# First layer of two in steps of one feature tile and a whole batch: wide y products and a block for the remaining tokens

## The chip, the cores and the metric

One core of a Trainium2 chip runs the whole program. The metric is the device time of one execution in microseconds. The kernel before took 1465.08 us (median of 3 runs, 1463.18 to 1466.22).

## What is computed

An attention with few keys in between, then two feed-forward layers:

```python
p_packed = softmax(p k^T / 8) v          # 8 batches, 8 heads, 32 packed rows, 576 tokens, 64 wide
out      = softmax(q p_packed^T / 8) p_packed
x  = out as [8*576, 512]
h1 = x @ w_in1                           # [4608, 512] x [512, 2048]
g1 = h1 - tanh(h1)
y  = g1 @ w_out1                         # [4608, 2048] x [2048, 512]
h2 = y @ w_in2
out = (h2 * cos(h2)) @ w_out2
```

The weights arrive as 64-bit values and are joined on the chip. Every large product is made from three: each operand is split into a rounded part (hi) and the remainder (lo), and hi*hi, lo*hi and hi*lo are added up in PSUM.

## The kernel before

**The first layer** never forms x. With the packed attention's second softmax `a` (32 keys for each of 8 heads, 576 tokens of a batch, `a2` in two halves) the layer's input product is `a` times `g`, where `g` is the packed values times `w_in1` (`gmat`, L521: 32 small products for a quarter c of the features, split by `gsplit_hi` and `gsplit_lo`, L540 and L547). A step n is one entry of the list `steps` (L1158): a block of 288 tokens (half a batch) and two tiles of 128 features. Its parts:

- `h1` (L564): 12 products of 288 columns on TensorE into one of two PSUM tiles `h` of two banks each. All attention pieces use the same two tiles.
- ScalarE: tanh `t` and square `u` of h (L588, L589), then `y` (L632) and the mask `k` (L635). Both feature tiles go through one instruction of 576 columns.
- VectorE: `t` = h - tanh (L637), `d` = u*h (L638), `gl` of the step before (L659), the polynomial `y` (L640), and a masked copy of `t` into `y` (L644). The result is g.
- ScalarE rounds g to `gh` in the next step (L652).
- `ymm1` (L661): 24 products of 288 columns, two steps later: 4 output tiles d, 2 feature tiles, 3 products. They add up in four PSUM banks over 8 steps, the 2048 features of a block.

The first four blocks go through the first half of the features and then through the second (`NP`, `HS`), with the half-sums stored to memory and added on VectorE (`ypart1` L683, `yload` L692, `yevac1` L699); so only half of the weights is needed early. Later blocks are evacuated by ScalarE, four times 288 columns (L709).

**What sets the order.** Each engine runs its queue in order. Up to step 14 the queues follow the list `START` (L39), partly left to the scheduler; then a loop (L1194) issues each step in the order of the code, with tables that say in which step which other piece stands: attention of the batch to come (`attention`, `ATT`, `PACK`, `G`, L72 to L75: scores in steps 0 and 1 of 16, transposes in 2 and 4, values in 3 and 5, the pack in 7, second scores in 8 and 10, gp groups in 9, 11, 13 and 15), joins of second-layer weights (`CONV2`, L64) and their sums (`SUM1`, L67, `combine_ops` L853). `GLENG` (L37) says which of the first 15 `gl` GpSimd takes.

**The second layer** begins with one block of 512 tokens: `h2` (L726) of the pair `ORDER2[0]` stands between the last two `ymm1` (L1261 to L1265), its cosine on ScalarE and VectorE beside the last y products. It then goes on for 8 steps and for pairs of blocks with fewer, combined products. All its products have 512 columns. Loads and stores are issued on SP's queue, in order.

The lines that say what a step is:

```python
steps = [(blk, HS * h + s) for h in range(2) for blk in range(NP) for s in range(HS)]
steps += [(blk, s) for blk in range(NP, NB) for s in range(NSTEP)]
```

## Time and profile before

| | us |
|---|---|
| median of 3 runs | 1465.08 |
| profiled execution | 1464.91 |
| its span, first to last instruction | 1463.1 |
| TensorE busy | 1419.1 |
| TensorE weight loads busy | 1238.8 |
| VectorE busy | 1226.7 |
| ScalarE busy | 987.8 |
| GpSimd busy | 125.1 |

The profile is of one execution. Busy time of TensorE contains the overlap of pipelined products, so the pace is read from the start of one group to the start of the next. The weight loads run beside the products. DVE is VectorE, ACT ScalarE, POOL GpSimd, PE TensorE, PEld its weight loads, SP the engine that issues the DMAs. The first layer reaches to about 760 us.

### The profile page before, as it was taken

How to read it: one execution, taken by the hardware profiler on the slowest of the kernel's cores; microseconds unless marked ns; L12 is line 12 of the kernel's file. 1: busy time of each engine (PE TensorE's matmuls, PEld its weight loads, DVE VectorE, ACT ScalarE, POOL GpSimd, SP SyncE). 2: the span in 40 equal slices, each digit the busy share in tenths (PEclk: the TensorE clock that was granted, in tenths of full speed). 3: DMA queues.
4: the chain of work that ended last, by engine and by line, in shares of the span. 5: the costliest groups of instructions: out<-in, count | busy, mean ns of one | idle time of the engine just before them, and what ended most of it. 6: DMA issues, size and time to landing. Idle time of an engine off the chain costs nothing.

```text
span 1463.1 us, 26436 instructions
## 1 busy us (share of the span) xinstructions
PE 1419.1 (97%) x9964; PEld 1238.8 (85%) x9964; DVE 1226.7 (84%) x1707; ACT 987.8 (68%) x1548; POOL 125.1 (9%) x102
## 2 busy tenths in 40 slices
PE   5899999999999999999999999999999999999998
PEld 2688989999899998999998888878887888788887
DVE  6898797898989889899867679997889689868975
ACT  4887666778787776878875566654665566646752
POOL 0311010111211111121130000000000000000000
PEclk6899999999999999999999999999999999999999
DMA  9742455737557583565679557787768776887566
GB/s 358 268 178 64 140 173 161 248 109 252 172 177 250 167 268 127 211 213 188 196 270 402 193 189 236 244 245 211 209 189 257 220 211 192 243 237 211 173 171 181
DMA packets 205119, 307.47 MB, mean 210 GB/s; under 512 B 48256, under 2 KB 135296, under 8 KB 204992
## 3 DMA queue, kind: packets, MB, share of 16 engines
q1 hardware_dynamic: 203904, 305.52, 64.8%
q8 instruction: 79, 1.29, 0.4%
q14 instruction: 48, 0.39, 0.1%
q10 hardware_dynamic: 1088, 0.26, 0.1%
HBM read 238.35 MB, written 67.37 MB: 209 GB/s over the span
## 4 chain that ended last, share of the span: by engine, by line
PE 89%; DVE 4%; DMA 4%; issue 2%; ACT 1%; SPq 0%; POOL 0%; DVEq 0%; POOLq 0%; ACTq 0%
PE y L673 26%; PE p L996 21%; PE y L1006 13%; PE h L573 13%; PE p L1006 5%; PE h L734 3%; PE y L810 3%; PE gp L530 2%; DMA st<-w1i 1%; DMA yw<-wso 1%; PE pp L406 1%; DMA v<-vv 1%; PE s L338 1%; DMA q<-qT 1%; PE sc L338 1%
## 5 line engine op out<-in xcount | busy, mean ns | idle before, releaser
L996 PE MATMUL p<-b,hw 128*128 128x512 f32 x1302 | 308.1, 389 | 0.0
L673 PE MATMUL y<-gh,w1o 128*128 128x288 f32 x2048 | 303.9, 300 | 3.7 <-DVE ye L703 2.3
L673 PEld LDWEIGHTS y<-gh,w1o 128*128 128x128 f32 x2048 | 278.3, 189 | 29.9 <-ACT t L588 14.9
L996 PEld LDWEIGHTS p<-b,hw 128*128 128x128 f32 x1302 | 244.3, 188 | 51.0 <-DVE hb L1013 0.3
L573 PE MATMUL h<-a,g 128*128 128x288 f32 x1536 | 227.3, 297 | 6.7 <-DVE g L549 4.2
L573 PEld LDWEIGHTS h<-a,g 128*128 128x128 f32 x1536 | 212.9, 190 | 8.8 <-issue 7.2
L588 ACT ACTIVATE t<-h 128x576 f32<-128x576 f32 x113 | 73.7, 652 | 145.9 <-PE h L573 145.9
L673 PE MATMUL y<-gl,w1o 128*128 128x288 f32 x1024 | 156.4, 294 | 0.0
L673 PEld LDWEIGHTS y<-gl,w1o 128*128 128x128 f32 x1024 | 143.1, 188 | 0.8 <-DVE u L450 0.4
L1006 PE MATMUL y<-yh,yw 128*128 128x512 f32 x376 | 120.0, 391 | 3.8 <-DMA yw<-wso 2.6
L659 DVE TENSOR_TENSOR gl<-y,gh 128x576 fp32r<-128x576 f32 x125 | 105.9, 847 | 3.5 <-ACT gh L652 3.4
L644 DVE COPY_PREDICATED y<-k,t 128x576 f32<-128x576 int16 x113 | 95.2, 842 | 10.7 <-DVE y L640 0.5
L637 DVE TENSOR_TENSOR t<-h,t 128x576 f32<-128x576 f32 x113 | 84.0, 744 | 21.7 <-ACT u L589 21.0
L1013 DVE TENSOR_TENSOR yl<-k,yh 128x1024 fp32r<-128x1024 f32 x72 | 86.7, 1214 | 17.7 <-ACT yh L1016 17.1
L652 ACT ACTIVATE gh<-y 128x576 fp32r<-128x576 f32 x128 | 88.1, 688 | 10.0 <-DVE y L644 5.4
L1006 PE MATMUL y<-gh,yw 128*128 128x512 f32 x256 | 91.1, 389 | 0.0
L1006 PEld LDWEIGHTS y<-yh,yw 128*128 128x128 f32 x376 | 70.6, 188 | 21.3 <-ACT o L1016 2.4
L1016 ACT ACTIVATE c<-p 128x512 f32<-128x512 f32 x96 | 56.9, 593 | 43.8 <-PE p L996 43.8
L640 DVE SCALAR_TENSOR_TENSOR y<-y,d 128x576 f32<-128x576 f32 x113 | 85.8, 759 | 0.0
L638 DVE TENSOR_TENSOR d<-u,h 128x576 f32<-128x576 f32 x113 | 83.9, 742 | 0.0
L1006 PE MATMUL p<-yh,yw 128*128 128x512 f32 x256 | 80.8, 389 | 0.5 <-DMA yw<-wso 0.5
L632 ACT ACTIVATE y<-u 128x576 f32<-128x576 f32 x113 | 77.2, 684 | 0.0
(186 smaller groups left out, 2389.3 us busy)
## 6 DMA issues: line engine op xcount, KB each, us to landing
yw<-wso SPq DMA_DIRECT2D x128, 256.0 KB, 3.1
hw<-wsi SPq DMA_DIRECT2D x124, 256.0 KB, 3.1
w1i<-w1d SPq DMA_DIRECT2D x48, 512.0 KB, 5.4
yw<-wod SPq DMA_DIRECT2D x96, 256.0 KB, 3.3
hw<-wid SPq DMA_DIRECT2D x93, 256.0 KB, 3.3
y<-ye SPq DMA_DIRECT2D x80, 144.0 KB, 1.9
st<-w1i SPq DMA_DIRECT2D x16, 512.0 KB, 8.1
v<-vv SPq DMA_DIRECT2D x16, 512.0 KB, 6.7
```

The source lines that it names most:

```text
L573: nc.tensor.matmul(out=h[:, x, 0:HB], lhsT=gw[b, f // 4, half][:, ga, c0:c0 + 128], rhs=a2[b, half][:, aa, HB * j:HB * j + HB], start=(n = ...
L632: nc.scalar.activation(out=y, in_=u, func=AF.Square, scale=PC2 ** 0.5, bias=PC1 / (2 * PC2 ** 0.5))
L637: lambda: nc.vector.tensor_tensor(out=t, in0=hs, in1=t, op=ALU.subtract),
L638: lambda: nc.vector.tensor_tensor(out=d, in0=u, in1=hs, op=ALU.mult),
L640: lambda: nc.vector.scalar_tensor_tensor(out=y, in0=y, scalar=PC0 - PC1 * PC1 / (4 * PC2), in1=d, op0=ALU.add, op1=ALU.mult,),
L644: lambda: nc.vector.copy_predicated(out=y, mask=k.bitcast(I16), data=t),
L652: nc.scalar.activation(out=st["gh"], in_=st["g"], func=AF.Copy)
L659: eng.tensor_tensor(out=st["gl"], in0=st["g"], in1=f32(st["gh"]), op=ALU.subtract)
L673: nc.tensor.matmul(out=yps[blk][d][:, 0:HB], lhsT=w1out[f][:, wh, 128 * d:128 * d + 128], rhs=st[gg][:, x, :], start=(s in first and x == ...
L996: nc.tensor.matmul(out=dst, lhsT=w[:, wi, 128 * j:128 * j + 128], rhs=b[j][bi], start=(first and n == 0), stop=(n == 5), skip_group_check= ...
L1006: nc.tensor.matmul(out=dst[d], lhsT=w[:, wi, 128 * d:128 * d + 128], rhs=src, start=(first and n == 0), stop=(n == 2), skip_group_check=True,)
L1013: nc.vector.tensor_tensor(out=out, in0=x, in1=y, op=op)
```

## The change

A step is now a whole batch (576 tokens in two halves of 288) and one feature tile of 128. `h1` makes the same 12 products of 288 columns, for two halves of one tile. The element operations keep their 576 columns. `ymm` makes 12 products of the first 512 tokens. The 64 tokens left (g, not yet rounded) go to memory by one store in each step (`el3`), into `rest[f]`, 8 batches side by side: 512 columns for each feature tile. Behind the last step a block `yrest` loads the 16 tiles (4 ahead), rounds and subtracts them (`split_rest`) and makes 16 x 12 products of 512 columns; the first `h2` of the second layer stands inside it, in the banks of y. The two halves of the features are now gone through for the first two batches. `START` names the order of the first 32 steps, all by hand. In the later steps the evacuation of gp stands earlier on ScalarE and ahead of the masked copy on VectorE. `GLENG` gives GpSimd 20 of the first 32 `gl` instead of 3 of 15. Four of the eight weight sums, and two weight loads, move from the steps to the block behind them (`SUMR`, `W2LOADR`); the second layer takes its pairs in order 0 to 7, the last two loaded as well.

```diff
-NSTART = 15
-GLATE = ([1, 2, 15], [1, 3, 22])
-DEPTH = 3
-GLENG = "VVVPVVPVVPVVVVV"
+NSTART = 32
+DEPTH = 2
+GLENG = "PPPPPVPVPPVPPPPVVPVPVVPVVPPVPPPV"
 START = (
...
-CONV2 = (34, 35, 37, 38) + tuple(16 * k + r for k in (3, 4, 5, 6) for r in (0, 2, 3, 5, 6))
-CONV2 += (112, 114, 116, 118, 120, 122, 124, 126)
-ORDER2 = (6, 7, 0, 1, 2, 3, 4, 5)
-SUM1 = {50: "i0", 66: "i1", 69: "o0", 82: "i2", 98: "i3", 101: "o1", 110: "i4", 113: "o2"}
+CONV2 = tuple(16 * k + r for k in range(2, 7) for r in (0, 2, 3, 6, 15)) + (112, 114, 115, 117, 119, 121, 123)
+ORDER2 = (0, 1, 2, 3, 4, 5, 6, 7)
+SUM1 = {51: "i0", 67: "i1", 83: "o0", 114: "i2"}
+SUMR = {0: "o1", 4: "i3", 8: "o2", 11: "i4"}
-W2LOAD1 = {124: 0, 125: 1, 127: 2}
-W2LOAD = {0: 3, 1: 4, 2: 5}
+W2LOAD1 = {127: 0}
+W2LOADR = {4: 1, 10: 2}
+W2LOAD = {0: 3, 1: 4, 2: 5, 3: 6, 4: 7}
-LOAD = (-4, 0, -3, 3, 0, 8)
+LOAD = (-4, -2, -3, 3, 0, 8)
-G = 9, 11, 13, 15
+G = 12, 14, 22, 25
+G2 = (2, 38), (3, 41)
+RRING = 4
+HAT = 5
...
+    rest = [dram.tile([128, B * TR], F32, name=f"rest{f}") for f in range(NF)]
...
-    def h1(blk, s, st):
-        b, j = divmod(blk, 2)
+    def h1(b, f, st):
         h = pss("h")
+        c0 = 128 * (f % 4)
         for x in range(2):
-            f = 2 * s + x
-            c0 = 128 * (f % 4)
...
-                        rhs=a2[b, half][:, aa, HB * j:HB * j + HB],
+                        rhs=a2[b, half][:, aa, HB * x:HB * x + HB],
...
-        st["y"] = mt("y", 2)
+        st["y"] = mt("y", 3)
...
     def el3(st):
         st["gh"] = mt("gh", 2, F32R)
         nc.scalar.activation(out=st["gh"], in_=st["g"], func=AF.Copy)
+        b, f = st["at"]
+        nc.sync.dma_start(out=rest[f][:, TR * b:TR * b + TR], in_=flat(st["g"])[:, TB:S])
...
+    def ymm(y, f, hi, lo, parts, first, last):
+        order = [(part, d) for part in parts for d in range(4)]
+        for part, d in sorted(order, key=lambda x: x[1]) if last else order:
+            for wh, gg in (((0, hi), (1, hi)) if part == 0 else ((0, lo),)):
+                nc.tensor.matmul(
+                    out=y[d], lhsT=w1out[f][:, wh, 128 * d:128 * d + 128], rhs=gg,
+                    start=(first and part == 0 and wh == 0), stop=(last and part == 1),
+                )
...
+    def load_rest(f):
+        t = wp.tile([128, 2, TB], F32, tag="w", name="r")[:, 0]
+        nc.sync.dma_start(out=t, in_=rest[f])
+        return t
+
+    def split_rest():
+        t, g = rests.pop(0), wtile("r")
+        nc.scalar.activation(out=g[:, 0], in_=t, func=AF.Copy)
+        nc.vector.tensor_tensor(out=g[:, 1], in0=t, in1=f32(g[:, 0]), op=ALU.subtract)
+        halves.append(g)
+
+    def yrest(fs):
+        if not yr:
+            yr.extend(t[:, i] for t in (pss("yr"), pss("yr")) for i in range(2))
+        for f in fs:
+            g = halves.pop(0)
+            ymm(yr, f, g[:, 0], g[:, 1], (0, 1), f == 0, f == NF - 1)
+            if f + RRING < NF:
+                rests.append(load_rest(f + RRING))
+            if rests:
+                split_rest()
+            for fn in rfill[f]:
+                fn()
...
-    steps = [(blk, HS * h + s) for h in range(2) for blk in range(NP) for s in range(HS)]
-    steps += [(blk, s) for blk in range(NP, NB) for s in range(NSTEP)]
+    steps = [(b, HF * h + f) for h in range(2) for b in range(NP) for f in range(HF)]
+    steps += [(b, f) for b in range(NP, B) for f in range(NF)]
...
     ymm1(*hist.pop(0))
...
     st0 = {}
-    h2(ORDER2[0], yt, st0)
+    yrest(range(2))
+    ymm1(*hist.pop(0))
+    yevac1(B - 1)
+    yrest(range(2, HAT))
+    h2(ORDER2[0], yt, st0, [psy.tile([128, TB], F32, tag="y", name="h") for _ in range(2)])
     cos_first(st0)
-    ymm1(*hist.pop(0))
-    yevac1(NB - 1)
+    yrest(range(HAT, NF))
+    yrest_evac()
```

Three places of the order. The first is TensorE in a later step with a transpose of the attention (`tp`); `h` are the first layer's h products, of which only the last and the first of a dozen are shown. Before:

```order
L573 MATMUL h<-a_7882,g 128x288
L380 MATMUL tp<-idn,e 128x128 x4
L380 MATMUL tp<-idn,e 64x128
L673 MATMUL y<-gh,w1o 128x288 x16
L673 MATMUL y<-gl,w1o 128x288 x8
L573 MATMUL h<-a_7731,g 128x288
```

And now:

```order
L601 MATMUL h<-a_6682,g 128x288
L402 MATMUL tp<-idn,e 128x128 x4
L402 MATMUL tp<-idn,e 64x128
L701 MATMUL y<-gh,w1o 128x512 x8
L701 MATMUL y<-gl,w1o 128x512 x4
L601 MATMUL h<-a_6553,g 128x288
```

Between two groups of h stand 12 y products of 512 columns where there were 24 of 288.

The second place is VectorE in the tenth step, from the masked copy of the ninth on (before) and from the tenth's `t` on (now); `wt` is a weight being joined. Before:

```order
L626 COPY_PREDICATED y<-k,t 128x576
L613 TENSOR_TENSOR t<-h,t 128x576
L617 TENSOR_TENSOR d<-u,h 128x576
L659 TENSOR_TENSOR gl<-y,gh 128x576
L621 SCALAR_TENSOR_TENSOR y<-y,d 128x576
L227 SCALAR_TENSOR_TENSOR wt<-wt,st 128x512
L626 COPY_PREDICATED y<-k,t 128x576
```

And now:

```order
L641 TENSOR_TENSOR t<-h,t 128x576
L645 TENSOR_TENSOR d<-u,h 128x576
L641 TENSOR_TENSOR t<-h,t 128x576
L649 SCALAR_TENSOR_TENSOR y<-y,d 128x576
L236 TENSOR_SCALAR wt<-wt 128x512
L242 SCALAR_TENSOR_TENSOR wt<-st,wt 128x512
L654 COPY_PREDICATED y<-k,t 128x576
```

The `gl` has left VectorE's queue here for GpSimd's, a join of two instructions stands where one of one stood, and the next step's `t` comes ahead of this step's `y`.

The third place is TensorE at the end of the first layer; `h<-yhl` is the second layer's `h2`. Before:

```order
L673 MATMUL y<-gl,w1o 128x288 x8
L734 MATMUL h<-yhl,w2i 128x512 x24
L673 MATMUL y<-gh,w1o 128x288 x16
L673 MATMUL y<-gl,w1o 128x288 x8
L734 MATMUL h<-yhl,w2i 128x512 x24
```

And now, from the last y product of the last step on:

```order
L701 MATMUL y<-gl,w1o 128x512
L701 MATMUL yr<-r,w1o 128x512 x36
L802 MATMUL h<-yhl,w_8657 128x512 x12
L802 MATMUL h<-yhl,w_8659 128x512 x12
L701 MATMUL yr<-r,w1o 128x512 x132
L802 MATMUL h<-yhl,w_8827 128x512 x12
```

The block's products (`yr`, 24 more of them ahead of the last step's y) surround the first `h2`, which reads loaded weights now.

## Rows read from the trace of the kernel before

**Rows 1.** The page, busy us, share of the span and instructions of each engine

```profile
PE 1419.1 (97%) x9964; PEld 1238.8 (85%) x9964; DVE 1226.7 (84%) x1707; ACT 987.8 (68%) x1548; POOL 125.1 (9%) x102
```

**Rows 2.** The page, the chain that ended last, shares by engine

```profile
PE 89%; DVE 4%; DMA 4%; issue 2%; ACT 1%; SPq 0%; POOL 0%; DVEq 0%; POOLq 0%; ACTq 0%
```

**Rows 3.** Busy time by stretches, first layer

```profile
core 0: us, PE busy (x) PEld busy (x) DVE busy (x) ACT busy (x) POOL busy (x), PEclk, DMA share, GB/s
0.00:33.00 33.00, 15.81 (x204) 6.12 (x204) 18.95 (x42) 15.66 (x29) 1.50 (x7) 0.69 0.96 352
...
64.00:112.00 48.00, 45.89 (x433) 42.31 (x431) 46.59 (x77) 43.31 (x81) 11.44 (x9) 1.00 0.50 176
...
498.00:587.00 89.00, 88.56 (x866) 82.52 (x865) 78.72 (x125) 67.19 (x124) 14.02 (x11) 1.00 0.58 195
...
676.00:714.00 38.00, 38.00 (x289) 38.00 (x289) 35.36 (x51) 32.33 (x59) 4.92 (x4) 1.00 0.59 196
```

**Rows 4.** Timeline of TensorE, a step without attention (start us, us, what)

```profile
691.96 2.28 PE L673 MATMUL y<-gh,w1o 128*128 128x288 f32 x16
...
695.13 1.75 PE L573 MATMUL h<-a,g 128*128 128x288 f32 x12
696.72 2.29 PE L673 MATMUL y<-gh,w1o 128*128 128x288 f32 x16
```

**Rows 5.** The chain that ended last in order of time, second layer

```profile
1018.22 5.44 PE p L996 x24
```

**Rows 6.** Timeline of TensorE, two idle spells in steps 16 to 31

```profile
136.52 0.72 PE L338 MATMUL sc<-k,pin 64*32 64x288 f32 x16 [1.84 <-issue]
...
218.54 2.35 PE L673 MATMUL y<-gh,w1o 128*128 128x288 f32 x16 [2.35 <-DVE ye L703]
```

**Rows 7.** Timeline of TensorE, a gp group and the y products behind it

```profile
645.45 1.09 PE L530 MATMUL gp<-w1i,pt 64*32 64x256 f32 x32
646.48 2.40 PE L673 MATMUL y<-gh,w1o 128*128 128x288 f32 x16
```

**Rows 8.** Timeline of ScalarE, evacuations of two blocks, one batch apart

```profile
549.42 1.33 ACT L709 ACTIVATE ye<-y 128x288 f32<-128x288 f32 x4
...
637.98 1.33 ACT L709 ACTIVATE ye<-y 128x288 f32<-128x288 f32 x4
```

**Rows 9.** Timelines of TensorE, ScalarE and VectorE, who reads one h

```profile
677.67 2.29 PE L673 MATMUL y<-gh,w1o 128*128 128x288 f32 x16
...
677.86 0.65 ACT L588 ACTIVATE t<-h 128x576 f32<-128x576 f32 x1 [0.72 <-PE h L573]
678.41 0.65 ACT L589 ACTIVATE u<-h 128x576 f32<-128x576 f32 x1
...
679.09 0.76 DVE L637 TENSOR_TENSOR t<-h,t 128x576 f32<-128x576 f32 x1 [0.34 <-ACT u L589]
679.76 0.74 DVE L638 TENSOR_TENSOR d<-u,h 128x576 f32<-128x576 f32 x1
```

**Rows 10.** The waits, whole span (us in total, times, longest)

```profile
DVE et L397 <- ACT et L394: 21.0, 14, 2.3
```

**Rows 11.** Stretch at the second layer's start; DMA issues; groups by line

```profile
757.00:813.00 56.00, 56.00 (x257) 46.81 (x256) 39.90 (x52) 33.19 (x40) 0.00 (x0) 1.00 0.89 333
...
yr<-y SPq DMA_DIRECT2D x4, 256.0 KB, 5.0
...
L722 ACT ACTIVATE yhl<-yr 128x512 fp32r<-128x512 f32 x4 | 2.3, 630 | 0.0
...
L549 DVE TENSOR_TENSOR g<-gp,g 128x512 fp32r<-128x512 f32 x64 | 41.0, 679 | 0.0
```

**Rows 12.** Timelines of GpSimd and VectorE, gl beside a GpSimd subtraction and alone

```profile
487.68 1.46 POOL L483 TENSOR_TENSOR a<-ut,a 128x576 fp32r<-128x576 f32 x1 [5.82 <-ACT a L477]
...
488.21 1.54 DVE L659 TENSOR_TENSOR gl<-y,gh 128x576 fp32r<-128x576 f32 x1
...
492.56 0.75 DVE L659 TENSOR_TENSOR gl<-y,gh 128x576 fp32r<-128x576 f32 x1
```

More of the change, by code (lines that the diff above doesn't have):

```diff
@@ L299, in load_qk @@
     def load_qk(nm, src, b, half):
-        t = att.tile([128, 4, HB], F32, tag=nm, name=nm)
+        t = att.tile([128, 4, HB], F32, tag=nm, bufs=2 if nm == "k" else 1, name=nm)
         nc.sync.dma_start(out=t, in_=src[b, half])
@@ L557, in gsplit, with at_g @@
                 fn(b, c, gp, half)
+    def at_g(n, b, c):
+        x = {}
+        early[n].append(lambda: x.update(r=gmat(b, c)))
+        for half in range(2):
+            mid_hi[n].append(lambda half=half: gsplit_hi(b, c, x["r"], half))
+            mid_lo[n].append(lambda half=half: gsplit_lo(b, c, x["r"], half))
+        mid[n - 2].append(lambda: load_w1(c))
     def at_pair(n, f, g, *args):
@@ new lines, in ymm1 @@
+    def ymm1(b, f, st, parts=(0, 1)):
+        conv.need(w1out, f)
+        first, last = (0, HF) if b < NP else (0,), (HF - 1, NF - 1) if b < NP else (NF - 1,)
+        if 0 in parts and f in first:
+            yps[b] = [psy.tile([128, TB], F32, tag="y", name="y") for _ in range(4)]
+        hi, lo = (flat(st[k]) if k in st else None for k in ("gh", "gl"))
+        ymm(
+            yps[b], f, hi and hi[:, 0:TB], lo and lo[:, 0:TB], parts, f in first, f in last
+        )
+    ypart, ngl = {}, [0]
@@ new lines, in ye2, with ypart1, yload @@
+    def ye2():
+        return [t[:, i] for t in [wp.tile([128, 2, TB], F32, tag="w", name="ye") for _ in range(2)] for i in range(2)]
+    def ypart1(b):
+        for d, ye in enumerate(ye2()):
+            nc.scalar.activation(out=ye, in_=yps[b][d], func=AF.Copy, scale=1.0 / TWO_PI)
+            nc.sync.dma_start(out=y0[d, :, b * TB:b * TB + TB], in_=ye)
+        del yps[b]
+    def yload(b):
+        ypart[b] = ye2()
+        for d, ye in enumerate(ypart[b]):
+            nc.sync.dma_start(out=ye, in_=y0[d, :, b * TB:b * TB + TB])
@@ new lines, in yrest_evac @@
+    def yrest_evac():
+        for d, ye in enumerate(ye2()):
+            if d % 2 == 0:
+                nc.scalar.activation(out=ye, in_=yr[d], func=AF.Copy, scale=1.0 / TWO_PI)
+            else:
+                nc.vector.tensor_scalar(
+                    out=ye, in0=yr[d], scalar1=1.0 / TWO_PI, scalar2=None, op0=ALU.mult
+                )
+            nc.sync.dma_start(
+                out=y1[d].rearrange("p (b n) -> p b n", n=S)[:, :, TB:S],
+                in_=ye.rearrange("p (b n) -> p b n", n=TR),
+            )
@@ L1079, in fused_kernel @@
     todo = {}
-    for b in range(2):
+    for b in range(3):
         for half in range(2):
```

164 lines of the change are left out of this document (78 added, 86 removed), and 46 rows, old and new, of the table START.

## The prediction

> **What bounds the kernel now.** I read the page's busy line first, then the chain of waits, then busy time by stretches, then single steps on the timeline. TensorE is busy 97% of the span, VectorE 84%, ScalarE 68% [rows 1], and TensorE carries 89% of the chain that ended last [rows 2]: what TensorE issues is the time, unless a stretch says otherwise. The stretches do say otherwise at the start [rows 3]. From 0 to 33 us TensorE is busy for 15.8 us, at a granted clock of 0.69, between its two levels of 1.2 and 2.4 GHz, while the DMA share is 0.96: the first loads set the pace. From 64 to 112 us VectorE is busy 46.6 of 48.0 us and TensorE waits here and there; that stretch is VectorE's. From there TensorE has no rest worth the name: in 498 to 587, one batch, it is busy 88.6 of 89.0 us with VectorE at 78.7, and in 676 to 714, eight steps without attention, 38.0 of 38.0 with VectorE at 35.4.
>
> A step is 12 h products, whatever attention piece falls there, and 24 y products. One group of 24 y starts at 691.96 and the h products behind it at 695.13: 3.17 us, 132 ns each at 288 columns. The next y group starts at 696.72, so 12 h take 1.59 us [rows 4]. Products of 512 columns appear in the second layer: 24 in 5.44 us, 226.7 ns each [rows 5]. Per column that is 0.459 ns at 288 and 0.443 at 512, so a wide product saves little over 3% of the same columns. The saving is real only because nothing else is slower by it.
>
> **The change part by part.** *The y products.* The order shows 3072 products of 288 columns gone and 1536 + 192 of 512 in their place; the h products stay 1536 of 288, now both halves of one feature tile instead of one half of two. 3072 x 132.1 = 405.8 us becomes 1728 x 226.7 = 391.7 us: 14 us less if TensorE never waits more than before. It doesn't fall evenly. Inside the 128 steps, y goes from 24 x 132.1 = 3.17 to 12 x 226.7 = 2.72 us, so a step is 0.45 us shorter (57.6 us in all). The block of remainders then gives back 192 x 226.7 = 43.5 us.
>
> *Steps 0 to 11.* VectorE's stretch ends at 112 us, about where step 11 is through. VectorE's five operations a step are the same 576 columns wide; up to the twelfth step the new order has 29 of the weight joins where it had 25, against which many of the gl subtractions go to GpSimd. I count 0 here. The bounds are 12 x 0.45 = 5.4 us gained, if VectorE is relieved, and 3 us lost, if the four joins (about 0.6 us each) come on top.
>
> *Steps 12 to 31.* TensorE's, 20 x 0.45 = 9.0 us gained. Two of its idle spells there hang on the order that is now written by hand: 1.84 us ahead of scores, and 2.35 us behind the evacuation of a half-sum on VectorE [rows 6]. Four evacuations of a block on VectorE (16 of 288 columns) become two of a batch (8 of 512), and the same wait exists; I take back half, 2 us, with bounds of 0 and 4. Two gp groups of batch 2 move from here to steps 38 and 41: 1.03 us from one place to the other [rows 7], no change in the sum.
>
> *Steps 32 to 127.* 96 x 0.45 = 43.2 us, if TensorE keeps the pace. A batch here takes 88.6 us between equal evacuations (549.42 to 637.98) [rows 8]; it would take 81.4. VectorE's 78.7 us a batch stay, so its share rises from 88% to 97%. A stretch of 93% cost TensorE nothing [rows 3], though without attention, which shares h's two buffers. The buffers give the slack: TensorE turns from h to y at 677.67, ScalarE's two readings of h start at 677.86 and 678.41, VectorE's at 679.09 and 679.76, and the buffer is free at 680.5, 2.8 us after h [rows 9]. With attention in a step the next h needs that buffer, and TensorE meanwhile has the attention piece (about 0.5 to 1.0 us) and now 2.72 us of y, so 3.3 to 3.8 us: 0.5 to 1.0 us of slack where there was 0.45 more. The place that I see overrun is the third step of a batch: the evacuation of the batch before, four of 512 columns at about 0.6 us each on ScalarE instead of four of 288 in 1.33 us together, stands ahead of that step's tanh, in a step in which VectorE also waits for ScalarE's copy of the transposed scores (14 times, 1.5 us each, in the trace) [rows 10]. I take 1 us for each of the five batches with attention and 0.5 for the last, 5.5 us in all; bounds 0 and 20 (the second rival). That leaves 37.7 us.
>
> *The rest block.* 43.5 us of TensorE, plus 1 us for its beginning and end. Every tile is loaded (256 KB, 5.0 us to landing for such a load), rounded by ScalarE (0.63 us) and subtracted by VectorE (0.68 us) [rows 11], each far below the 2.72 us that a tile takes on TensorE, and loads run four tiles, 10.9 us, ahead. Four of the eight second-layer weight sums move here from the steps, and two of the 2 MB weight loads; the first second-layer h group stands inside the block in the freed y banks, so its sine work is covered as it was by y before. Bounds 43.5 and 51 (third rival).
>
> *What else is added.* 128 stores of 64 columns, one a step, on SP's queue. Each waits for VectorE's masked copy; behind it wait loads that are due steps later and stores that nobody waits for. The third buffer for g covers the store's landing. I cost both at nothing; if the cover went, a load late by one step would show as a TensorE wait of some us, which the upper bound of the steps holds. The partial sums of two batches are 512 columns instead of four blocks' 288: fewer bytes, nothing on TensorE. Last, five weight loads of 2 MB instead of three follow in the second layer's first pass, each due three steps of 48 x 226.7 ns = 10.9 us later; at the 333 GB/s of [rows 11] one takes 6.3 us, so they stay hidden: nothing.
>
> *GpSimd's share of gl.* 17 more of the gl subtractions go to GpSimd. In the trace such help is not free: the GpSimd subtraction from 487.68 to 489.14 met a gl on VectorE that took 1.54 us instead of 0.75 [rows 12]. So one moved gl frees 0.7 us and can cost 0.8; I take nothing for it. The Trainium skill (SBUF — State Buffer, Who interferes with whom) says that a VectorE instruction with two SBUF inputs and a GpSimd instruction that reads SBUF exclude each other for the whole instruction; the trace agrees, 0.79 us beside 1.46. By that rule each move makes VectorE lose as much as it gains wherever its next operation has two SBUF inputs; what that gives is the last rival.
>
> **Sum.** Profiled execution: 1464.9 us, span 1463.1 (the median of the runs shown is 1465.1, so the same). 1464.9 - 0 - 9.0 - 2.0 - 37.7 + 44.5 = 1460.7, said as 1461.
>
> **The rivals.** *VectorE takes over the attention steps: slower.* Place: steps 32 to 111. For it: 97% of a batch on VectorE, in order, with 13 of 16 steps whose next h needs VectorE's two subtractions done; and steps 0 to 11 show what happens when VectorE leads. Against it: 93% cost nothing in rows 3, and the joins and sums fall between attention pieces. It decides once VectorE is late by more than the 0.5 to 1.0 us of slack in most of these steps. At 0.3 us for each of the 13, a batch loses 4 us, five lose 20 where I have 5.5: 1475, and 1468 to 1483 for half and one and a half of it.
>
> *The rest block is starved.* In its 43.5 us pass twelve remainders (3.1 MB), two weight loads (4.2 MB), four sums in (2.1 MB) and out (4.2 MB): 313 GB/s, and in 757 to 813 the queue was at 0.89 with 333 GB/s [rows 11]. A 2 MB weight load is four of 512 KB, 6.3 us at that rate, and remainders queue behind it; with the wait for free buffers ahead of it the 10.9 us of lead can be used up. Two such misses of 3 us: 1467.
>
> *The start gains too.* If the new order fills VectorE better, steps 0 to 11 give their 5.4 us and the remaining idle some 4 more: 1451.
>
> *GpSimd blocks VectorE early.* Five of the moved gl colliding in VectorE's stretch at 0.8 us: 4 us back, 1465.
>
> That the change does not do what it says is ruled out by the counts in the order.
>
> **How the numbers follow.** Forecast (1455 to 1466) 0.43, VectorE leads 0.27, starved rest 0.13, better start 0.11, GpSimd 0.06. A measurement here can tell 0.2%, 2.9 us: faster is below 1462.2, slower above 1468.0. Three quarters of the forecast and all of the better start are faster, with a little of the starved rest: 0.44. A quarter of the forecast, GpSimd and some of the starved rest are the same: 0.23. The others are slower: 0.33. The range takes in the better start's 1451 and VectorE's case to just above its middle: 1449 to 1477, leaving out some 0.03 below and 0.12 above. The forecast's own range is 1455 to 1466.
>
> **What would show it.** Right: y groups of 12 in 2.72 us, batches of 82 to 83 us between evacuations, step 32's h at 214 to 219 us instead of 228, a rest block of 43.5 to 45 us without idle TensorE. VectorE leading: idle before h behind VectorE's d, batches of 85 us or more. Starved rest: idle before yr on r or its load. Wrong altogether: y at 512 columns costing more than 226.7 ns beside the busy weight loads, or VectorE's operations longer than now.

## The result and the profile after

The changed kernel takes 1484.71 us (median of 4 runs, 1482.27 to 1487.89) where the kernel before took 1464.13 in the same comparison: a ratio of 1.0142, with an interval of 1.0115 to 1.0168. That is 20.6 us slower. The prediction had said 1461 with a range to 1477; its slowest rival had said 1475. The profiled execution took 1486.03 us, with a span of 1484.2 where before had 1463.1.

The page of the changed kernel, busy us, share of the span and instructions, which answers to [rows 1]:

```profile
PE 1423.0 (96%) x8620; PEld 1156.0 (78%) x8620; DVE 1226.0 (83%) x1707; ACT 996.6 (67%) x1531; POOL 142.8 (10%) x113
```

VectorE is as busy as before, ScalarE 8.8 us busier. TensorE has fewer products, and should have been busy for 14 us less; it is busy for 3.9 us more in a span that is 21.1 us longer, so it also waits 17 us more. Where the time went is read from marks: the starts of the same product groups in both kernels. The timelines of TensorE, of before and then of the changed kernel, at h of steps 0, 12, 16, 32, 48, 112 and 127 and at the second `h2` of the second layer (start us, us, what):

```profile
33.09 3.22 PE L573 MATMUL h<-a,g 128*128 128x288 f32 x12 [4.22 <-DVE g L549]
...
106.34 1.76 PE L573 MATMUL h<-a,g 128*128 128x288 f32 x12
...
132.94 1.74 PE L573 MATMUL h<-a,g 128*128 128x288 f32 x12
...
227.80 1.74 PE L573 MATMUL h<-a,g 128*128 128x288 f32 x12
...
316.44 1.74 PE L573 MATMUL h<-a,g 128*128 128x288 f32 x12
...
671.33 1.74 PE L573 MATMUL h<-a,g 128*128 128x288 f32 x12
...
742.89 1.76 PE L573 MATMUL h<-a,g 128*128 128x288 f32 x12
...
759.50 5.62 PE L734 MATMUL h<-yhl,w2i 128*128 128x512 f32 x24
```

```profile
39.69 3.22 PE L601 MATMUL h<-a,g 128*128 128x288 f32 x12 [1.40 <-DVE g L571]
...
114.02 1.83 PE L601 MATMUL h<-a,g 128*128 128x288 f32 x12 [1.32 <-DVE d L645]
...
138.18 2.02 PE L601 MATMUL h<-a,g 128*128 128x288 f32 x12
...
225.95 1.82 PE L601 MATMUL h<-a,g 128*128 128x288 f32 x12
...
314.50 1.74 PE L601 MATMUL h<-a,g 128*128 128x288 f32 x12
...
646.39 1.75 PE L601 MATMUL h<-a,g 128*128 128x288 f32 x12
...
717.22 1.76 PE L601 MATMUL h<-a,g 128*128 128x288 f32 x12
...
781.22 5.62 PE L802 MATMUL h<-yhl,w 128*128 128x512 f32 x24
```

The difference of two neighbouring marks, after less before, against what the prediction's terms give for the same stretch. The last column is the same from a second profile of the changed kernel, the control below; it shows how far a stretch scatters. Counted in the traces, two gp groups fewer (2.06 us) stand in steps 12 to 15 and two more in 112 to 126; the forecast has them where they stand.

| stretch | forecast | measured | second profile |
|---|---|---|---|
| to the first h | 0 | +6.6 | +7.0 |
| steps 0 to 11 | 0 | +1.1 | +1.1 |
| steps 12 to 15 | -3.9 | -2.4 | -2.4 |
| steps 16 to 31 | -9.2 | -7.1 | -9.2 |
| steps 32 to 47 | -6.2 | -0.1 | -0.3 |
| steps 48 to 111 | -24.8 | -23.0 | -22.5 |
| steps 112 to 126 | -4.2 | -0.7 | +0.6 |
| h of step 127 to the second h2 | +44.1 | +47.4 | +47.2 |
| the rest | 0 | -0.6 | 0.0 |
| sum | -4.2 | +21.1 | +21.5 |

Steps 48 to 111 do nearly what was forecast. Of the 25 us that were missed, 7.7 are there at h of step 12, and 6.6 of these ahead of the first h. The others lie mostly in steps 12 to 47, in the last batch and in the block. Ahead of the first h the change holds more than the excerpt of its diff shows: a weight tile is loaded ahead of the first keys (`LOADS`), the weights come in another order and are joined another way (`ORDER`, `SPLIT`), and parts of the softmax change engines (`ATTENG`). The first scores start at 6.17 us instead of 4.20, and the first gp products at 35.08, behind the join of a weight. The waits, from TensorE's timeline of the changed kernel (in the brackets the idle time before the group and what ended it):

```profile
35.08 1.96 PE L552 MATMUL gp<-w1i,pt 64*32 64x256 f32 x32 [4.58 <-DVE wt L236]
...
84.02 3.34 PE L701 MATMUL y<-gh,w1o 128*128 128x512 f32 x8 [4.17 <-ACT gh L683]
...
97.07 0.82 PE L601 MATMUL h<-a,g 128*128 128x288 f32 x2 [3.77 <-DVE g L571]
...
199.71 0.90 PE L428 MATMUL pp<-v,et 128*32 128x64 f32 x40 [1.94 <-DMA v<-vv]
...
230.71 0.72 PE L360 MATMUL sc<-k,pin 64*32 64x288 f32 x16 [2.94 <-issue]
231.36 3.66 PE L701 MATMUL y<-gh,w1o 128*128 128x512 f32 x8
...
677.35 0.67 PE L552 MATMUL gp<-w1i,pt 64*32 64x256 f32 x16 [1.55 <-DMA w1i<-w1d]
...
777.24 4.14 PE L701 MATMUL yr<-r,w1o 128*128 128x512 f32 x10 [1.86 <-DVE r L751]
```

Some of these waits cost more than their length. The eight y products at 231.36 last 3.5 us to the next group instead of 1.87. Busy time by stretches around them, and around an idle spell of 2.35 us of the kernel before [rows 6], shows why; the last columns are PEclk, DMA share and GB/s:

```profile
202.00:204.00 2.00, 2.00 (x6) 1.61 (x5) 1.17 (x2) 0.00 (x0) 1.18 (x1) 0.50 0.17 61
...
230.00:232.00 2.00, 1.29 (x18) 0.76 (x19) 1.09 (x3) 1.59 (x3) 0.00 (x0) 0.83 0.49 152
232.00:234.00 2.00, 2.00 (x6) 1.61 (x5) 1.97 (x5) 0.67 (x2) 0.00 (x0) 0.50 1.04 357
234.00:236.00 2.00, 2.00 (x9) 1.59 (x8) 1.90 (x3) 1.31 (x4) 0.00 (x0) 0.82 0.79 313
```

```profile
218.00:220.00 2.00, 1.46 (x11) 1.49 (x12) 2.00 (x6) 1.91 (x4) 1.15 (x1) 1.00 0.36 117
```

TensorE idled for 2.94 us up to 230.71, and the granted clock was 0.83, 0.50 and 0.82 in the three rows from 230 us on; 0.50 is the lower level of 1.2 GHz. This gives the 1.6 us on the eight products. Behind the idle spell of before the clock stayed at 1.00. Behind the spells at 84, 97, 200 and 777 us a row of 2 us also goes down to 0.50 or 0.51.

The wait of 1.86 us at 777 us ends with a subtraction of a remainder (`r`), and VectorE's timeline shows what that stood behind: the pieces `cs` of a weight sum, of which the first waited 7.01 us for its load `cw`.

```profile
775.02 0.43 DVE L938 TENSOR_TENSOR cs<-cw 128x256 f32<-128x256 f32 x1 [7.01 <-DMA cw<-rawi]
...
776.50 0.68 DVE L751 TENSOR_TENSOR r<-r 128x512 fp32r<-128x512 f32 x1
```

The start in the busy times by stretches, to be held against [rows 3]:

```profile
0.00:33.00 33.00, 12.77 (x188) 4.90 (x188) 17.75 (x41) 15.24 (x27) 5.98 (x11) 0.75 0.97 350
...
64.00:112.00 48.00, 35.92 (x269) 27.63 (x268) 42.50 (x68) 38.09 (x68) 16.28 (x12) 0.89 0.56 193
...
498.00:587.00 89.00, 88.83 (x740) 71.84 (x739) 82.71 (x135) 72.36 (x129) 14.15 (x11) 1.00 0.65 217
```

From 64 to 112 us TensorE is busy for 10 us less, but VectorE (46.59 before) and ScalarE (43.31) are less busy too. In the batch from 498 to 587 us VectorE is busy at 93% and TensorE does not wait.

Last, the pace of the y products, in two steps and in the block:

```profile
712.82 1.75 PE L601 MATMUL h<-a,g 128*128 128x288 f32 x12
714.42 2.03 PE L701 MATMUL y<-gh,w1o 128*128 128x512 f32 x8
716.28 1.09 PE L701 MATMUL y<-gl,w1o 128*128 128x512 f32 x4
717.22 1.76 PE L601 MATMUL h<-a,g 128*128 128x288 f32 x12
...
733.94 8.34 PE L701 MATMUL yr<-r,w1o 128*128 128x512 f32 x36
742.12 5.60 PE L802 MATMUL h<-yhl,w 128*128 128x512 f32 x24
```

Twelve y of 512 columns take 2.80 us, 233.3 ns each, and a step 4.40. The 36 of the block take 8.18, 227.2 each, with the same weights and the same order. The forecast had 226.7 for both [rows 5].

### The profile page after: what moved, and what is told of

Read it like the earlier page. It is cut to its first block, busy times and chain, and to the rows that moved or that the text cites. A ratio compares the mean times of both kernels' runs of the same rounds, so it can differ in the third digit from the quotient of the medians.

```text
span 1484.2 us, 24020 instructions
## 1 busy us (share of the span) xinstructions
PE 1423.0 (96%) x8620; PEld 1156.0 (78%) x8620; DVE 1226.0 (83%) x1707; ACT 996.6 (67%) x1531; POOL 142.8 (10%) x113
## 4 chain that ended last, share of the span: by engine, by line
PE 44%; DMA 3%; DVE 3%; issue 3%; ACT 1%; POOL 1%; SPq 0%; DVEq 0%; ACTq 0%; POOLq 0%
PE p L1064 21%; PE y L1074 12%; PE p L1074 5%; PE h L802 3%; PE y L878 3%; PE yr L701 1%; DMA yw<-wso 1%; DVE yl L1081 1%; DMA yw<-wod 1%; DMA cw<-rawi 0%; DVE k L1081 0%; DMA rawi<-wt 0%; DMA rawo<-wt 0%; DMA cw<-rawo 0%; ACT yh L1084 0%
## 5 line engine op out<-in xcount | busy, mean ns | idle before, releaser
L701 PE MATMUL y<-gh,w1o 128*128 128x512 f32 x1024 | 275.2, 408 | 5.6 <-ACT gh L683 4.6
L701 PEld LDWEIGHTS y<-gh,w1o 128*128 128x128 f32 x1024 | 186.7, 191 | 67.2 <-issue 10.6
L701 PE MATMUL y<-gl,w1o 128*128 128x512 f32 x512 | 145.2, 399 | 0.3 <-POOL gl L692 0.3
L701 PEld LDWEIGHTS y<-gl,w1o 128*128 128x128 f32 x512 | 95.4, 189 | 23.8 <-issue 1.3
L616 ACT ACTIVATE t<-h 128x576 f32<-128x576 f32 x96 | 62.9, 655 | 69.7 <-PE h L601 69.4
L692 DVE TENSOR_TENSOR gl<-y,gh 128x576 fp32r<-128x576 f32 x108 | 93.5, 865 | 5.3 <-PE y L701 4.7
L675 DVE COPY_PREDICATED y<-k,t 128x576 f32<-128x576 int16 x96 | 79.4, 827 | 6.6
L667 DVE TENSOR_TENSOR t<-h,t 128x576 f32<-128x576 f32 x96 | 71.0, 740 | 14.8 <-ACT u L617 14.6
L1084 ACT ACTIVATE yh<-k 128x1024 fp32r<-128x1024 f32 x72 | 73.1, 1048 | 5.5 <-DVE k L1081 5.5
L1074 PE MATMUL y<-yl,yw 128*128 128x512 f32 x188 | 73.2, 389 | 0.0
L670 DVE SCALAR_TENSOR_TENSOR y<-y,d 128x576 f32<-128x576 f32 x96 | 71.8, 748 | 0.0
```

Of the source, the lines that this page charges most:

```text
L616: nc.scalar.activation(out=st["t"], in_=h, func=AF.Tanh)
L667: lambda: nc.vector.tensor_tensor(out=t, in0=hs, in1=t, op=ALU.subtract),
L670: lambda: nc.vector.scalar_tensor_tensor(out=y, in0=y, scalar=PC0 - PC1 * PC1 / (4 * PC2), in1=d, op0=ALU.add, op1=ALU.mult,),
L675: lambda: nc.vector.copy_predicated(out=y, mask=k.bitcast(I16), data=t),
L692: eng.tensor_tensor(out=st["gl"], in0=st["g"], in1=f32(st["gh"]), op=ALU.subtract)
L701: nc.tensor.matmul(out=y[d], lhsT=w1out[f][:, wh, 128 * d:128 * d + 128], rhs=gg, start=(first and part == 0 and wh == 0), stop=(last and ...
```

## The experiments

The theory after this reading: the steps themselves are as forecast but for the pace of y; the loss is made of single waits at places where the order was written anew, some made dearer by the clock behind them. The rivals: GpSimd's gl and VectorE's load make the waits; SP's queue of stores makes them; or the waits are only the visible end of a bound that takes any order. All ratios are to the kernel before, with 95% intervals. The changed kernel once more, as a control:

> The changed kernel itself once more, as a measure of how far its time scatters. Every theory expects 1482 to 1488 (ratio 1.012 to 1.017) and the same waits at the same places of the trace.

1.0144 (1.0130 to 1.0158), 1481.5 to 1486.4 us. So an edit of 2 to 4 us is hardly seen in the time; it is read in the trace. The trace scatters too: the wait for v is 1.36 us here without a fall of the clock, and steps 16 to 31 are 2.1 us shorter.

**No gl on GpSimd.**

```diff
-GLENG = "PPPPPVPVPPVPPPPVVPVPVVPVVPPVPPPV"
+GLENG = ""
```

> All gl subtractions on VectorE, none on GpSimd. If GpSimd's gl are what delays the first 32 steps (collisions of 0.7 to 1.1 us each with VectorE, and the masked copy of 1.59 us ahead of step 32), the idle of 4.17 us before the y of the sixth step and the 2.94 us before the scores of step 32 shrink by half or more, h of step 32 comes at 220 us or earlier instead of 226, and the time falls by 5 to 10 us against 1484.7. If VectorE itself is the limit of the start, 20 more operations of 0.75 us on it (15 us) make h of step 32 come at 230 to 240 us, and the time rises by 5 to 15 us.

1.0138 (1.0124 to 1.0151): neither. The waits are nearly the same, and so is the start (h of step 32 at 225.5 us instead of 226.0). TensorE's timeline and the stretch of the start:

```profile
83.38 3.62 PE L701 MATMUL y<-gh,w1o 128*128 128x512 f32 x8 [4.25 <-ACT gh L683]
...
96.58 0.82 PE L601 MATMUL h<-a,g 128*128 128x288 f32 x2 [3.90 <-DVE g L571]
...
229.73 0.72 PE L360 MATMUL sc<-k,pin 64*32 64x288 f32 x16 [2.44 <-issue]
```

```profile
64.00:112.00 48.00, 36.84 (x267) 28.17 (x266) 44.09 (x72) 38.20 (x69) 11.37 (x8) 0.86 0.58 198
```

Four gl came back to VectorE here, 3.0 us at 0.75 each, and its busy time rose by 1.6. Of the other 1.4, 1.1 are one join of a weight, which takes 0.69 us here and took 1.80 beside a gl on GpSimd. And 1.6 us more on VectorE cost nothing, so the changed kernel's start is not bound by VectorE's work, as I had taken it. That rests on this run and not on the stretch before.

**Only the two gl with the worst collisions moved.**

```diff
-GLENG = "PPPPPVPVPPVPPPPVVPVPVVPVVPPVPPPV"
+GLENG = "PPPPVVPVPPVPPPPVVPVPVVPVVPPVPPVV"
```

> Only the gl of the fifth step and of the 31st go from GpSimd to VectorE. GpSimd theory: these two collisions (two joins of 1.47 and 1.80 us instead of 0.41 and 0.69; a masked copy of 1.59 instead of 0.8) start the two worst idle spells; the joins of the fifth step last 0.4 and 0.7 us again, the 2.94 us of idle before the scores of step 32 fall to about 2 or less, and the time falls by 3 to 8 us. Rival (the spells come from the order in which the attention pieces stand, whatever GpSimd does): they stay within 1 us of what they were, and the time within 2 us of 1484.7.

1.0143 (1.0129 to 1.0157). The wait ahead of step 32 went from 2.94 to 2.44 us, that of 4.17 to 4.25. The rival holds.

**The 64-column stores on ScalarE's queue.**

```diff
-        nc.sync.dma_start(out=rest[f][:, TR * b:TR * b + TR], in_=flat(st["g"])[:, TB:S])
+        nc.scalar.dma_start(out=rest[f][:, TR * b:TR * b + TR], in_=flat(st["g"])[:, TB:S])
```

> The 128 stores of the 64 remaining columns are issued by ScalarE, right behind the rounding that has waited for the same g, instead of on SP's queue. If the stores on SP hold up the loads behind them, the gp products of the last batch no longer wait for their weights (0.50 and 1.55 us in the changed kernel), the 1.94 us wait for v near 200 us goes, and the time falls by 3 to 6 us. If those loads are late because they are issued late and share the bandwidth, these waits stay and the time is within 2 us of 1484.7.

1.0121 (1.0101 to 1.0141). Both waits of the last batch's gp are gone, and h of step 112 to h of step 127 takes 68.8 us instead of 70.8:

```profile
645.48 1.75 PE L601 MATMUL h<-a,g 128*128 128x288 f32 x12
...
714.27 1.75 PE L601 MATMUL h<-a,g 128*128 128x288 f32 x12
```

All profiles with the stores on SP, the control's too, lie between 69.7 and 72.7, all with them on ScalarE between 68.3 and 68.8. So the stores on SP did delay these loads. For v it is not shown: 1.15 us instead of 1.94, but 0.88 to 2.85 in the other profiles with the stores on SP. And the edit seems to have a price: steps 48 to 111 take 333.0 us, where the profiles with the stores on SP have 331.3 to 332.6 but for one, and h waits 1.7 us for VectorE's d instead of 0.7 from 250 to 640 us.

**The last weight sum one tile later.**

```diff
-SUMR = {0: "o1", 4: "i3", 8: "o2", 11: "i4"}
+SUMR = {0: "o1", 4: "i3", 8: "o2", 12: "i4"}
```

> The last weight sum of the rest block is loaded one tile later, so its VectorE operations stand behind the last subtraction of a remainder. If the idle of 1.86 us before the last yr products (and the half clock behind it, some 1.7 us) comes from VectorE waiting in order for the sum's load, both go: the block takes 43.5 to 45 us between its ends without the last y and h2, and the time falls by 3 to 4 us. If the remainder's own load or rounding is late, the idle stays and the time is within 1 us of 1484.7.

1.0136 (1.0113 to 1.0159). The wait inside the block is gone, and another takes its place behind it, where the second `h2` needs the banks that the block's sums are read from:

```profile
777.99 2.37 PE L802 MATMUL h<-yhl,w 128*128 128x512 f32 x9 [2.17 <-DVE ye L772]
```

So the cause of the wait is shown, but no gain: from the block's first product to that h2 it is 54.2 us instead of 55.6, and 53.7 to 55.8 in the profiles that leave the sum where it was. Behind these 2.17 us the clock stays at 1.00.

**The pool of the step's tiles without its shift of 64 bytes.**

```diff
-    shift(mp, 64)
```

> The 64 bytes that shift the pool of the step's tiles (t, u, k, d, y, gh, gl) are left out, so gh and gl begin at multiples of 128 bytes, as the operands of the rest block and of the second layer do. In the changed kernel a y product of 512 columns in a step takes 233 ns, one of the rest block 227. If the address of gh and gl is the cause, y falls to 227 ns, 1536 x 6.6 ns = 10 us less: 1475. If it is the company (VectorE and ScalarE reading at the same time, the change from h to y), y stays at 233 and the time within 2 us of 1485; what the shift was good for elsewhere could then make it slower.

1.0147 (1.0130 to 1.0164). Twelve y took 2.78 instead of 2.80 us: the address to 128 bytes is 1.6 of the 6 ns.

**The gp group's evacuation ahead of step 32 moved up.**

```diff
-... Z29 P31 G30 K31 L30 R31 M31 gm21 gt21 gs21 gl21 gk21
+... Z29 gm21 P31 gt21 gs21 gl21 gk21 G30 K31 L30 R31 M31
```

> In the order of the start, the last gp group's evacuation (its two roundings on ScalarE, its two subtractions on VectorE) stands ahead of the rounding of the 31st step's g, the mask of the 32nd and the masked copy of the 32nd, instead of behind them. Theory (the scores of step 32 wait for the gp tile's buffer, which is freed by these subtractions): they end at about 228.5 instead of 230.6 us, the idle of 2.94 us falls below 1, the granted clock does not fall behind it, and the time falls by 3 to 5 us. Rival (the scores wait for something else): idle as before, time within 2 us of 1485.

The trace does what the theory said. The scores' wait is 0.69 us, though the next scores wait 1.65, and the clock stays up. TensorE's timeline, and the stretch (0.79 in the changed kernel):

```profile
227.05 0.72 PE L360 MATMUL sc<-k,pin 64*32 64x288 f32 x16 [0.69 <-PE h L601]
...
234.18 0.72 PE L360 MATMUL sc<-k,pin 64*32 64x288 f32 x16 [1.65 <-ACT e L388]
```

```profile
228.00:236.00 8.00, 6.35 (x45) 4.68 (x44) 5.63 (x11) 5.63 (x11) 0.00 (x0) 1.00 0.72 252
```

From h of step 32 to h of step 48 it takes 86.7 us instead of 88.6 (88.4 in the control). The time, 1.0135 (1.0118 to 1.0153), does not show 2 us.

**The start, four ways.** Step 5's polynomial and masked copy ahead of batch 1's softmax on VectorE:

```diff
-... Q5 E5 L4 c sm10 a s211 U6 D6 Z4 i su11 Q6 sb10 P5 se10 sm11 a R5 i sn10 sb11 G5 K6 E6 Y5 ...
+... Q5 E5 L4 P5 R5 G5 c sm10 a s211 U6 D6 Z4 i su11 Q6 sb10 se10 sm11 a i sn10 sb11 K6 E6 Y5 ...
```

> In the order of the start, VectorE's polynomial and masked copy of the sixth step stand ahead of four operations of batch 1's second softmax instead of behind them, and its rounding on ScalarE likewise; no work is added or left out. Theory (the order of VectorE's queue makes the first great idle spell): the y products of the sixth step start at 80 to 81 us instead of 84.0, the idle of 4.17 us falls below 2, the clock stays up there, h of step 8 comes 1 to 3 us earlier, and the time falls by 2 to 4 us. Rival (the spell is only moved: the softmax that now stands behind delays h of step 8 by as much): idle before h of step 8 grows by 2 to 3 us and the time is within 2 us of 1485.

1.0154 (1.0132 to 1.0175). The y products start at 80.15 as expected, and the wait comes back in pieces (1.12 and 2.99 us, at 83 and 88 us, and 2.19 instead of 0.97 before gp); h of step 8 starts 1.7 us later. The rival holds. Next, the loads and the first gp in another order:

```diff
-ORDER = "i1 o5 i2 o0 i3 o3 i0 o1 ...
+ORDER = "i1 i2 i3 i0 o0 o5 o3 o1 ...
...
-... sc11 sn01 c st00 sx11 sh00 sp01 a so00 i st01 a ex10 b W8 i sh01 b gm00 ex11 rc10 so01 c rc11 tr10 gt00 gs00 gk00 a gl00 i te10 H0 ...
+... gm00 sn01 st00 sh00 gt00 gs00 sp01 a so00 gl00 gk00 i st01 sh01 so01 ex10 sc11 sx11 H0 a b W8 i ex11 b rc10 c rc11 tr10 c a i te10 c ...
```

> The start is put into another order: the four input weights of the first quarter are loaded and joined ahead of three output weights, the first gp group and its evacuation stand ahead of batch 1's second scores, batch 0's last softmax operations go to VectorE, and the first h stands ahead of batch 1's transposes. Theory (the first h comes 6.6 us later than before because of the order of the loads and of the queues, and all of the first 16 steps carry that): the first h starts at 33 to 36 us instead of 39.7, h of step 16 comes 3 to 5 us earlier than 138.2, and the time falls by 2 to 5 us. Rival (the steps that follow wait for later weights and for batch 1 anyway): the first h comes earlier, h of step 8 stays at 96 to 97 us, and the time is within 2 us of 1485.

1.0149 (1.0132 to 1.0166). The first h starts at 36.29 us instead of 39.69, and h of step 8 at 99.91 instead of 97.07: what this order put behind the first h comes back there. So an earlier first h is not enough by itself. Whether the late one is what the later steps carry stays open; no run puts the loads and the softmax of the kernel before (`LOADS`, `ORDER`, `ATTENG`) back. Next, batch 1's second softmax without its maximum, which leaves out its subtraction too (the exponentials are of the scores themselves):

```diff
         def sm(js=(0, 1)):
-            x["m", js] = stat("m", js, ALU.max)
+            if b != 1:
+                x["m", js] = stat("m", js, ALU.max)
...
-            apply(js, x["m", js], ALU.subtract, 0)
+            if b != 1:
+                apply(js, x["m", js], ALU.subtract, 0)
```

> In batch 1's second softmax the maximum and its subtraction are left out (a reduction on VectorE and a subtraction on GpSimd or VectorE for each of two halves of the heads; the exponentials are taken of the scores themselves). Theory (h of step 8 ends a chain through that softmax): the chain is 2 to 4 us shorter, h of step 8 starts at 93 to 95 us instead of 97, and the time falls by 2 to 4 us. Rival (h of step 8 waits for the input weights of that batch's gp groups, or for VectorE's queue behind them): it stays at 96 to 97 us, time within 2 us of 1485.

1.0145 (1.0131 to 1.0159). The wait of 4.17 fell to 2.95 us, and h of step 8 stands at 97.11: the rival. Last, batch 1's second gp group behind step 8's h:

```diff
-... gt10 gm11 L6 K7 st11 a gk10 gs11 b i P7 sh11 b W18 gt11 gl11 so11 sh10 gk11 gs10 so10 gl10 a R7 H8 ...
+... gt10 gs10 L6 K7 st11 a gk10 gl10 b i P7 sh11 so11 sh10 so10 H8 b W18 gm11 a R7 i G7 b gt11 gs11 gl11 gk11 ...
```

> In the order of the start, the second gp group of batch 1 and its evacuation (features of the steps from the 13th on) stand behind the h of step 8 instead of ahead of it; batch 1's first gp evacuation and last softmax operations move up, the third batch's first scores move behind the ninth step's elementwise work. No work is added. Theory (h of step 8 waits for a chain through the two shared PSUM buffers, h of step 7, gp, gp, h, and for the evacuations that stand ahead in ScalarE's and VectorE's queues): h of step 8 starts at 92 to 95 us instead of 97, the idle of 3.77 us ahead of it falls below 2, h of step 16 at 133 to 136 instead of 138.2, and the time falls by 2 to 5 us. Rival (the whole start is bound by the sum of work on VectorE and ScalarE, so that any order moves the wait only): h of step 16 stays within 1 us of 138.2, the time within 2 us of 1485.

1.0176 (1.0157 to 1.0195), slower. Step 8's h starts at 94.32 us, 2.75 earlier, as the theory had it, but h of step 12 at 118.3 instead of 114.0 and h of step 16 at 142.5 instead of 138.2:

```profile
94.32 1.33 PE L600 MATMUL h<-a,g 128*128 128x288 f32 x4 [4.34 <-ACT a L498]
...
102.50 0.50 PE L700 MATMUL y<-gh,w1o 128*128 128x512 f32 x1 [2.32 <-ACT w1o L269]
```

The y products now wait for an output weight whose rounding stands behind the moved evacuation on ScalarE.

**Where the y products read.** gh and gl in wider tiles, without the shift:

```diff
+    def mt2(tag):
+        t = mp.tile([128, 960], F32R, tag=tag, bufs=2, name=tag)
+        return t[:, 0:S].rearrange("q (a n) -> q a n", a=2)
...
-        st["gh"] = mt("gh", 2, F32R)
+        st["gh"] = mt2("gh")
...
-            st["gl"] = mt("gl", 2, F32R)
+            st["gl"] = mt2("gl")
...
-    shift(mp, 64)
```

> gh and gl lie in tiles of 960 elements (the 576 in front are used) and without the 64 bytes of shift. If the width of the tile that a product's columns are read from makes 233 ns of 227, y in the steps falls towards 227 ns and the time by up to 10 us. If not, y stays at 232 to 233 ns as it did without the shift alone, and the time within 2 us of 1485.

1.0139 (1.0120 to 1.0157); twelve y in 2.78 us again. And gh and gl laid first in the pool, 17 KB lower:

```diff
-    shift(mp, 64)
+    for tag in ("gh", "gl"):
+        t0 = mp.tile([128, 2, HB], F32, tag=tag, bufs=2, name="low")
+        nc.gpsimd.memset(t0, 0.0)
```

> gh and gl are laid first in the pool of the step's tiles, without the 64 bytes of shift, so that they lie where the second layer's own gh and gl lie later (some 17 KB lower than in the changed kernel); t, u, d and y move up. If the place in memory makes a y product take 233 ns, y falls to 227 ns and the time by 7 to 10 us. If not, y stays at 232 to 233 ns, time within 2 us of 1485.

The pace follows the place, though t, u, d and y lie elsewhere too:

```profile
709.76 1.74 PE L601 MATMUL h<-a,g 128*128 128x288 f32 x12
711.35 2.00 PE L701 MATMUL y<-gh,w1o 128*128 128x512 f32 x8
713.18 1.07 PE L701 MATMUL y<-gl,w1o 128*128 128x512 f32 x4
714.09 1.74 PE L601 MATMUL h<-a,g 128*128 128x288 f32 x12
```

Twelve y take 2.74 us, 228 ns each. But the time is 1.0146 (1.0127 to 1.0164), unchanged: h of step 48 to h of step 112 takes 331.3 us instead of 331.9. The y products of these 64 steps took 184.1 us instead of 186.2, about half of what 0.06 us a step would give, because behind an attention piece they gained less (behind gp 239 instead of 242 ns). And TensorE's idle time there rose from 0.8 to 2.4 us: most of what the products give comes back as waits.

**Edits together.** The stores, the sum and the evacuation ahead of step 32 (the three edits above):

> Three edits together: the stores of the 64 columns issued by ScalarE, the last weight sum of the rest block one tile later, and the last gp group's evacuation of the start ahead of the step's other work. Each took a wait away in its own trace (2 us before the last batch's gp, 1.9 us in the rest block, 2.9 us ahead of step 32). If they add up, the time falls by 5 to 9 us, to 1476 to 1480. If the waits are only moved, it is within 3 us of 1485.

1.0099 (1.0085 to 1.0114), 1478.60 us. The intervals of this and of the control don't meet: the three edits together give 6.6 us. In the trace the gain stands in two stretches: steps 32 to 47 take 85.0 us instead of the control's 88.4 (the 1.65 us that the second scores waited with the evacuation alone are gone too), and steps 112 to 126 take 68.8 instead of 72.2. The block, 54.1 us, is within its scatter. With step 8's order and with the last value products of the start behind two groups of y:

```diff
-... G26 pp21 R27 U28 T28 Z24 E28 K28 px21 D28 Q28 L26 Y25 P28 pk2 Z25 ...
+... G26 R27 U28 T28 Z24 E28 K28 D28 Q28 L26 Y25 pp21 P28 px21 pk2 Z25 ...
```

> The three edits of the run before that gave 1478.6, with this order of the second gp group and with the last value products of the start (which waited 1.5 to 2.5 us for v) behind two groups of y instead of ahead of them. If the waits are independent, 1471 to 1476; if the start's order gives nothing, 1476 to 1479. Below 1465 would need more than the waits that the traces show outside the y products' own pace.

1.0131 (1.0115 to 1.0148): the order of step 8 takes back what the others gave (h of step 16 at 143.7 us instead of 138.5). So that order was dropped:

> The three edits that gave 1478.6, and the last value products of the start behind two groups of y instead of ahead of them; the gp groups as in the changed kernel. In the run with five edits the wait for v was gone. If that wait (1.5 to 2.5 us, and the half clock behind it) counts, 1474 to 1477; if the time is taken up by a later wait, 1477.5 to 1480.

1.0097 (1.0082 to 1.0112), 1478.57 us. Against the run with three edits the wait for v is gone, and h of step 16 to h of step 32 takes 84.6 us instead of 85.8; the clock from 180 to 250 us was 1.00 in both. The time, 1478.57 beside 1478.60, does not show it. The last run adds the low place of gh and gl:

> The four edits that gave 1478.6, and gh and gl laid first in their pool (y at 228 to 230 instead of 233 ns). If TensorE is the only bound of the steps, the 128 steps are 5 to 7 us shorter and the time is 1471 to 1474. If VectorE stands right behind TensorE there (as the run with the low place alone suggests: products faster, time unchanged), waits of h for VectorE take most of it and the time is 1476 to 1479.

1.0083 (1.0069 to 1.0097), 1476.35 us, the best of the changed versions. Its interval overlaps the one before. The waits and the busy time from 250 to 640 us:

```profile
PE h L600 <- DVE d L667: 2.3, 8, 0.5
```

```profile
250.00:640.00 390.00, 386.36 (x3147) 313.61 (x3146) 359.02 (x572) 309.66 (x551) 68.99 (x53) 1.00 0.59 201
```

Steps 48 to 111 take 332.0 us, where the run with four edits took 333.3. The y products of these steps are 2.7 us shorter, and TensorE's idle time is 1.4 us longer; of the 2.3 us of waits for VectorE's d above, 2.0 were there with four edits. So about half of what the products give is kept here. No version beats the kernel before.

## Why the prediction was wrong

**Steps 0 to 11: "I count 0 here" failed**, with bounds of -5.4 and +3: h of step 12 comes 7.7 us later than before. 6.6 of them are there at the first h. The sum has no term for the stretch ahead of it: I had read it as set by the first loads, and took no account of the new order of these loads and of the queues. From the first h to step 12 it is 1.1 us more, with 8 groups of y in it instead of 9. There I had called the stretch VectorE's because it was busy for 46.6 of 48 us before, and counted VectorE's operations. In the changed kernel VectorE is less busy (42.5) and TensorE waits more, and 1.6 us more of VectorE's work cost nothing (the run without gl on GpSimd). So a count of work does not give the time of the start. That the new order costs by what stands behind what, in four in-order queues and two shared h buffers, is argued from the waits; which link decides is not settled. An earlier step 5, an earlier first h, a shorter softmax and an earlier step 8 each took time from the place that they aimed at, and none gave an earlier step 16.

**Steps 12 to 47: "20 x 0.45" failed, and the 1 us of waits for the batch behind step 32.** The two idle spells of before went whole (4.2 us, of which I had taken back half), so that term erred on the safe side. But two others came, for v (1.94 us) and ahead of step 32 (2.94 us), and behind both the clock fell and cost 1.6 to 1.7 us more, a price that no term held. With the slower y they make up most of the 3.6 us missed in steps 12 to 31 and of the 6.1 in 32 to 47. In the control the wait for v is shorter and the clock stays up, and steps 12 to 31 miss 1.5. The run with the evacuation moved up shows the cause of the second: the scores' buffer is freed by a gp evacuation that the new order put behind a step's other work. Why v comes late is open.

**"226.7 ns each" for y was mis-sized**: 233.3 in the steps, 0.08 us a step, 10.2 us over 128. I had taken the pace from the second layer [rows 5]. The prediction had named a dearer y as what would make it wrong altogether. It did less than that: where it was had back (228), waits took half and more of it.

**Steps 48 to 111: the mechanism was right, and the number in part luck.** A batch takes 83.0 us (331.9 for four) against 82.5 by the terms. But of the 4 us of waits that I expected in these four batches about 1 came, and the slower y gave 5: two errors offset each other. The heavier rival, VectorE over the limit, did not come: TensorE waits 0.7 us for VectorE's d from 250 to 640 us. But VectorE is close behind, at 92%, as the waits in the runs with the low place or with the stores on ScalarE show. I had given it 1475 and 0.27, and the time came out slower still for other reasons.

**Steps 112 to 127: "I cost both at nothing" failed** for the stores on SP's queue. Moved to ScalarE's queue, they no longer hold up the last batch's weights, and 2.0 us come back (3.4 against the control). The prediction had named the sign, a load late by one step; it had put it into the bound and not into the sum.

**The rest block: 44.5 was mis-sized**, 48.6 measured (64.00 us from h of step 127 to the second h2, less 15.4 for h, three y groups and h2). Over the profiles that leave its order as it is, it is 46.7 to 49.0. 192 x 227 ns are 43.5; the beginning waited 1.00; the last ten products waited 1.86 and took 3.98 instead of 2.27, at a clock of 0.50 and 0.78 in the rows from 778 to 782 us. The rival of the starved block had the right place and the wrong cause: not the remainder's load was late, but its subtraction, which stood on VectorE behind a weight sum that waited for its own load; the wait inside the block went when that sum was moved.

**GpSimd's share: "I take nothing for it" held.** With all gl on VectorE the time is the same (1.0138 beside the control's 1.0144). The Trainium skill (SBUF — State Buffer, Who interferes with whom) says that a VectorE instruction with two SBUF inputs and a GpSimd instruction that reads SBUF shut each other out; the trace agrees: a masked copy of 1.59 us instead of 0.8 beside a gl on GpSimd, and 3.0 us of gl that came back to VectorE and raised its busy time by 1.6.

The forecast's sum thus failed mostly in what it left out. It priced the products and the operations, and took the rewritten order, at the start and at the places where the work changes hands, at nothing. Some 7 to 9 of the 25 us that were missed are taken out by edits of single places; the rest is located in the traces, and its causes stay in part open.

## To carry to other kernels

A saving on the engine that bounds the steady state says nothing about the stretches in which an order is written by hand: there a new order has to be read row by row, for what each buffer's release stands behind. An idle spell of TensorE can cost half of its length or more again by the clock behind it (1.6 us behind 2.94, 1.7 behind 1.86; nothing behind 2.35 in the kernel before), so price it with the products that follow. And where a change adds small stores to a queue that also issues loads, look for the load that is due soonest behind them, or issue the store from the engine that has already waited for its data, and look what that costs there.
